# Moving a long convolution's x and result through memory channel by channel, with a deeper buffer for its inverse

## The chip, the cores and the metric

The program runs on one core of one Trainium2 chip. The metric is the device time of one execution in microseconds (us), as the median of several. The engines are TensorE (PE, matmuls; its weight loads are shown as PEld), VectorE (DVE), ScalarE (ACT), GpSimd (POOL) and SyncE (SP, which issues the DMAs here).

## The reference, cut to what matters

A long convolution gates its input, and two feed-forward layers follow it, token by token (S = 12480 tokens, D = 128 channels, FF = 2048):

```python
h = (relu(pos_emb @ w1) @ w2) * exp(-0.01 * pos)[:, None]
y = irfft(rfft(x * v, 2 * S) * rfft(h, 2 * S))[:S]      # over the tokens
t = x * y
h1 = t @ w_in1
P = a0 + a1 * h1 + a2 * h1**2 + a3 * h1**3
Q = 1 + abs(b0) * abs(h1) + abs(b1) * h1**2
t = (P / (Q + 1e-6)) @ w_out1
h2 = t @ w_in2
out = maximum(0.01 * h2, h2) @ w_out2
```

## The kernel before, in words

The first part (up to about 327 us) makes the transform of x * v and of h, multiplies them, and stores an intermediate `bd` in device memory. The second part, called the main part here, takes the last step of the inverse transform and both layers, tile by tile. A tile is five columns n of a 98 x 128 arrangement of the tokens, 490 or 486 tokens wide; tile 0 has three columns, 294 tokens; there are 26 tiles. In the main part a tile's numbers stand with the 128 channels on the partitions and the tokens along the row.

The steps of the main part have short names, and a table gives each to an engine:

- For each tile: `xP` (PE) transposes the tile's x from token rows (`xc`) into PSUM, five transposes; `xA` (ACT) copies it to SBUF. `yP` (PE) makes the inverse's result y with ten matmuls, each of which is two instructions in the trace, from `bt` (a part of `bd`) and the table `dt`; `yA` (ACT) copies it to SBUF. `yG` (POOL) multiplies x and y into `zf`; `zA` and `zG` split that into a high and a low part for three-pass matmuls. For tile 0 `yP` is called `wP`, and DVE does what POOL does for the others.
- Layer 1, for each of 16 blocks of 128 hidden units (a unit): `h1` (PE, three passes of one instruction each), then a chain over ACT, DVE and POOL that makes P / Q: `s`, `v`, `rho`, `r0` on ACT, `q`, `p`, `N` on POOL, `nn`, `d`, `ee`, `e`, `g` on DVE; `o1` (PE) adds the block to the tile's result. `g` is the chain's last step, and it is what `o1` waits for.
- Between the layers `uA`, `uB` (ACT) and `uG` (POOL) split the result of layer 1.
- Layer 2, for each of 16 units: `h2` (PE, three passes), `rl` (ACT), and `o2` (PE). In the four units that `CG` lists, `rh` (ACT) and `rg` (POOL) split the block and `o2` is done in three passes.
- At the end of a tile `oA` (ACT) copies the result to `o2s`; `oP` (PE) transposes it back in groups of four columns n, `oB` (ACT) copies that to `ot`, and SP stores token rows. There are 32 such groups.

The order on each engine is fixed before the program runs. `plan` (line 198) goes through the steps with a cost (`cost`, line 76) and a lag (`lag`, line 97) for each, and gives an engine that is free the ready step with the lowest number: the step's unit number plus its kind's entry in `PLACE` (line 55). `BUF` (line 47) has the number of buffers of each kind, and `work_list` (line 105) turns them into dependences. `h1`, `h2`, `xP`, `yP` and `oP` share three PSUM banks (`NHB`). Every engine then goes through its list in that order, and waits where an input isn't there. SP's DMAs stand in the order in which the steps that issue them come: the inputs of tile j + 2 are issued when both `xP` and `yP` of tile j have been recorded (`loaded`, line 928), since the buffers of `dt`, `xc` and `bt` are two each.

```python
def loaded(j, i):
    T["yin", j][i] = None
    if T["yin", j][0] is T["yin", j][2]:
        load_y(j + BUF["in"])
```

Of the kernel before, what the change touches and what calls it, by code (L numbers as in the profile page):

```python
# [75 lines left out]
def cost(k, w):  # L76
# [13 lines left out]
    if k in ("wP", "yP"):  # L90
        return w * 4.32
    if k == "xP":
        return w * 0.855
    return {"oP": 432, "oB": 478}[k]
# [10 lines left out]
def work_list(tiles):  # L105

    nt = len(tiles)
    off = [sum(tiles[:j]) for j in range(nt + 1)]
# [54 lines left out]
    for j in range(nt):  # L163
        w, b, n = COLS[j], j * NF, j * NF + NF - 1
        i = j - BUF["in"]
        load = [("xP", i, 7000), ("yP" if i else "wP", i, 7000)] if i >= 0 else []
# [8 lines left out]
        if j:
# [130 lines left out]
def conv_moe_moe(ctx: ExitStack, tc: tile.TileContext, I, out, dbg=None):  # L306
# [50 lines left out]
    xe, ve, oute = ends(x), ends(v), ends(out)  # L357

    with tc.manual_schedule():
# [549 lines left out]
        def load_y(j):  # L909
# [16 lines left out]
            T["yin", j] = [bt, dt, xc]

        def loaded(j, i):

            T["yin", j][i] = None  # L930
            if T["yin", j][0] is T["yin", j][2]:
                load_y(j + BUF["in"])

        def x_pe(j):
            t, xc = bank("xP", j), T["yin", j][2]
            for i in range(TILES[j]):
                c = cols(j, i)
                m = c.stop - c.start
                pe.transpose(t[:, c], xc[:m, i], ident[:m, :m])
            loaded(j, 2)  # L940
# [122 lines left out]
        def o_pe(b):
            t = bank("oP", b)
            for i in range(OB):
                n = b * OB + i
                j = max(k for k in range(len(TILES)) if OFF[k] <= n)
                c, m = cols(j, n - OFF[j]).start, ROW[n]
                pe.transpose(t[:m, i * D : (i + 1) * D], T["o2s", j][:, c : c + m], ident)

        def o_act2(b):
            n0 = b * OB
            ot = mp.tile([NU, OB, D], F32, tag="ot", name=f"ot{b}")
            m = ROW[b * OB]
            act.copy(ot[:m], T.pop(("oP", b))[:m].rearrange("p (i d) -> p i d", d=D))
            for sl, k, a, b in token_rows(n0, n0 + OB):
# [46 lines left out]
```

## Time and profile before

| | us |
|---|---|
| median of 3 runs | 1648.87 |
| lowest and highest run | 1644.95 and 1650.23 |
| the profiled execution, its own time | 1647.39 |
| the profiled execution, span from first to last instruction | 1645.6 |

The profile is of one execution. A busy PE in it is not PE at its peak: matmuls are pipelined and their ends are modelled, so a matmul's own duration is longer than the distance from its start to the next one's. This distance (the pitch) is what one instruction costs a PE that never waits.

### The profile page before, as it was taken

To read this page: it belongs to the slowest core of one execution; us is meant where nothing else is said; L and a number is where in the kernel's file an instruction comes from. 1 tells how busy PE (TensorE), PEld (TensorE's weight loads), DVE (VectorE), ACT (ScalarE), POOL (GpSimd) and SP (SyncE) were. 2 spreads that over 40 slices of the span, in tenths; PEclk is the share of its full clock that TensorE was granted. 3 is DMA by queue.
4 is the path that set the end of the run, shared out by engine and by line. 5 is a ranking of instruction groups with operands and counts; after the bars stand their busy time and mean duration, and the time that the engine had idled before them with its cause. 6 is when DMAs were issued, how large, how long until landed. Compare 5 with 4: busy or idle time off the path is not lost.

```text
span 1645.6 us, 21850 instructions
## 1 busy us (share of the span) xinstructions
PE 1588.4 (97%) x6568; PEld 1138.0 (69%) x6568; DVE 1459.0 (89%) x2401; ACT 1360.2 (83%) x2671; POOL 1391.5 (85%) x1187
## 2 busy tenths in 40 slices
PE   7889989888999999999999999999999999999998
PEld 5778888675666666666666666666666666666665
DVE  5878766579999999999999999999999999999991
ACT  4672483378999999999999999999999999999994
POOL 6637526588999999999999999999999999999992
PEclk9999999989999999999999999999999999999999
DMA  7846556541010111001110001110011110000000
GB/s 211 247 137 199 194 164 243 175 106 27 8 30 18 31 32 32 19 18 31 32 32 25 25 19 31 32 37 14 19 31 32 37 31 6 1 6 10 5 6 15
DMA packets 89048, 97.33 MB, mean 59 GB/s; under 512 B 53092, under 2 KB 58446, under 8 KB 87762
## 3 DMA queue, kind: packets, MB, share of 16 engines
q1 hardware_dynamic: 88010, 95.54, 19.9%
q8 instruction: 52, 0.85, 0.2%
q10 hardware_dynamic: 920, 0.40, 0.1%
q14 instruction: 66, 0.54, 0.1%
HBM read 70.84 MB, written 25.07 MB: 58 GB/s over the span
## 4 chain that ended last, share of the span: by engine, by line
PE 86%; DMA 5%; DVE 3%; POOL 2%; SPq 1%; issue 1%; ACT 1%; ACTq 0%; DVEq 0%; POOLq 0%
PE o1p L992 20%; PE o2p L992 15%; PE h L495 11%; PE h L497 11%; PE h L496 11%; PE xp L688 4%; PE yP L947 4%; PE gp L723 2%; PE ap L648 2%; PE gp L719 2%; DMA A<-x 1%; PE o2p L495 1%; PE o2p L497 1%; PE o2p L496 1%; DMA wk<-v 1%
## 5 line engine op out<-in xcount | busy, mean ns | idle before, releaser
L1028 POOL TENSOR_TENSOR wk<-wk 128x972 f32<-128x972 f32 (+2 forms) x208 | 470.0, 2260 | 23.7 <-DVE wk L1025 21.2
L992 PE MATMUL o1p<-g,wo 128*128 128x486 f32 (+2 forms) x832 | 405.6, 571 | 6.4 <-DVE g L1043 6.4
L1019 POOL TENSOR_SCALAR wk<-wk,pars 128x486 f32<-128x486 f32 (+2 forms) x416 | 314.3, 756 | 35.5 <-ACT wk L1011 20.8
L1030 DVE SCALAR_TENSOR_TENSOR v<-wk,absb,v 128x486 f32<-128x486 f32 (+2 forms) x416 | 297.1, 714 | 11.5 <-ACT v L1013 10.5
L1037 DVE SCALAR_TENSOR_TENSOR v<-v,r 128x486 f32<-128x486 f32 (+2 forms) x416 | 274.0, 659 | 33.3 <-ACT r L1035 30.7
L992 PE MATMUL o2p<-wk,wo 128*128 128x486 f32 (+2 forms) x624 | 301.6, 566 | 0.0
L1013 ACT ACTIVATE v<-h,absb 128x486 f32<-128x486 f32 (+2 forms) x416 | 267.4, 645 | 13.3 <-DVE g L1043 10.2
L1025 DVE TENSOR_TENSOR wk<-h,wk 128x486 f32<-128x486 f32 (+2 forms) x416 | 270.8, 651 | 0.5 <-POOL wk L1019 0.2
L1040 DVE SCALAR_TENSOR_TENSOR v<-v,r 128x486 f32<-128x486 f32 (+2 forms) x416 | 266.5, 659 | 4.7
L1011 ACT ACTIVATE wk<-h 128x486 f32<-128x486 f32 (+2 forms) x416 | 240.1, 577 | 35.4 <-PE h L497 29.5
L1033 ACT ACTIVATE rho<-v 128x486 f32<-128x486 f32 (+2 forms) x416 | 241.4, 580 | 24.0 <-DVE v L1030 23.4
L1035 ACT ACTIVATE r<-rho 128x486 f32<-128x486 f32 (+2 forms) x416 | 255.9, 615 | 3.6
L1043 DVE TENSOR_TENSOR g<-wk,v 128x486 f32<-128x486 f32 (+2 forms) x416 | 253.7, 649 | 4.0 <-POOL wk L1028 2.5
L495 PE MATMUL h<-zh,wh 128*128 128x486 f32 (+2 forms) x416 | 253.9, 610 | 3.3 <-DVE wk L1025 2.3
L1050 ACT ACTIVATE wk<-h 128x486 f32<-128x486 f32 (+2 forms) x416 | 242.0, 582 | 12.4 <-PE h L497 11.5
L1021 POOL TENSOR_SCALAR wk<-wk,pars 128x972 f32<-128x972 f32 (+2 forms) x208 | 239.6, 1152 | 0.0
L992 PEld LDWEIGHTS o2p<-wk,wo 128*128 128x128 f32 x624 | 117.8, 189 | 109.9 <-issue 104.6
L495 PE MATMUL h<-uh,wh 128*128 128x486 f32 (+2 forms) x416 | 187.6, 451 | 0.9 <-ACT wk L1050 0.9
L992 PEld LDWEIGHTS o1p<-g,wo 128*128 128x128 f32 x832 | 154.6, 191 | 47.0 <-issue 14.8
L497 PE MATMUL h<-zh,wl 128*128 128x486 f32 (+2 forms) x416 | 159.8, 384 | 0.0
L496 PE MATMUL h<-zl,wh 128*128 128x486 f32 (+2 forms) x416 | 159.7, 384 | 0.0
L497 PE MATMUL h<-uh,wl 128*128 128x486 f32 (+2 forms) x416 | 158.9, 382 | 0.0
(105 smaller groups left out, 2558.5 us busy)
## 6 DMA issues: line engine op xcount, KB each, us to landing
bd<-wk SPq DMA_DIRECT2D x44, 256.0 KB
bt<-bd SPq DMA_DIRECT2D x100, 112.5 KB
wk<-c_m SPq DMA_DIRECT2D x43, 256.0 KB
dt<-c_d SPq DMA_DIRECT2D x25, 344.5 KB
A<-x SPq DMA_DIRECT2D x32, 192.0 KB
wk<-v SPq DMA_DIRECT2D x32, 192.0 KB
out<-ot SPq DMA_DIRECT2D x32, 192.0 KB
xc<-x SPq DMA_DIRECT2D x25, 240.0 KB
```

Source lines behind the costliest of these rows:

```text
L495: pe.matmul(dst, w_h, z_h, start=start, stop=False)
L496: pe.matmul(dst, w_h, z_l, start=False, stop=False)
L497: pe.matmul(dst, w_l, z_h, start=False, stop=stop)
L992: pe.matmul(o, wo[l][:, f], T.pop((src, n))[:, :w], start=(f == 0), stop=(f == NF - 1))
L1013: act.activation(bank("v", n)[:, :w], one("h1"), AF.Abs, scale=kk)
L1019: pool.tensor_scalar(out=q, in0=sq, scalar1=a3, scalar2=a1, op0=ALU.mult, op1=ALU.add)
L1025: dve.tensor_tensor(out=half("nn"), in0=one("h1"), in1=two("q"), op=ALU.mult)
L1028: pool.tensor_tensor(out=nn, in0=nn, in1=T["p", n][:, : 2 * w], op=ALU.add)
L1030: dve.scalar_tensor_tensor(out=one("v"), in0=two("s"), scalar=bb, in1=one("v"), op0=ALU.mult, op1=ALU.add)
L1035: act.activation(mk("r0"), one("rho"), AF.Square)
L1037: dve.scalar_tensor_tensor(out=one("v"), in0=one("v"), scalar=C1, in1=one("r0"), op0=ALU.add, op1=ALU.mult)
L1040: dve.scalar_tensor_tensor(out=one("v"), in0=one("v"), scalar=-2.0, in1=one("r0"), op0=ALU.add, op1=ALU.mult)
```

## The change

x comes to the program a second time, as `xm`: 128 channels by 12480 tokens and a few columns of padding, in the order in which the tiles take them. The host writes this array before the launch, and puts the result, which now leaves as 128 channels by tokens in the same order, back into token rows after it. x as it was is still loaded for x * v in the first part.

So `xP`, `xA`, `oP` and `oB` are gone. A tile's x is one DMA straight into the buffer that `yG` reads (`xt`, three buffers), issued when `yG` of the tile three before is recorded; a tile's result is one DMA from `o2s`. The inputs `dt` and `bt` of tile j + 2 are issued right after `yP` of tile j. `yA` has 14 buffers in place of 4. The three-pass units of layer 2 are 0, 5, 7 and 13 in place of 1, 5, 9 and 13, and `PLACE` has other numbers.

```diff
+LEFT = [sum(COLS[:j]) for j in range(len(COLS) + 1)]
...
-    "s": 3, "q": 3, "p": 2, "nn": 3, "rho": 2, "r0": 3, "g": 3, "rl": 3, "rh": 2, "rd": 2, "zf": 2, "xA": 4, "yA": 4, "in": 2,
+    "s": 3, "q": 3, "p": 2, "nn": 3, "rho": 2, "r0": 3, "g": 3, "rl": 3, "rh": 2, "rd": 2, "zf": 2, "xA": 3, "yA": 14, "in": 2,
...
-CG = [1, 5, 9, 13]
+CG = [0, 5, 7, 13]
...
-    "N": -942.49, "d": -98.01, "e": 2053.67, "ee": -1296.06, "g": -1349.74, "go": -2822.11, "h1": -2.6, "h2":
+    "N": -5165.29, "d": -98.77, "e": 794.99, "ee": -3335.26, "g": -3628.59, "go": -7712.1, "h1": -2.6,
...
-    "P": "h1 h2 o1 o2 wP yP xP oP",
-    "A": "s v rho r0 rl rh yA xA zA uA uB oA oB",
+    "P": "h1 h2 o1 o2 wP yP",
+    "A": "s v rho r0 rl rh yA zA uA uB oA",
...
-        load = [("xP", i, 7000), ("yP" if i else "wP", i, 7000)] if i >= 0 else []
+        load = [("yP" if i else "wP", i, 7000)] if i >= 0 else []
...
-            op("yG", j, w, b, [("yA", j), ("xA", j)] + zf)
+            op("yG", j, w, b, [("yA", j)] + zf + ([("yG", j - BUF["xA"], 5000)] if j > BUF["xA"] else []))
...
-        op("oA", j, w, n + NF, [("o2", n)] + ([("oP", (off[j - 1] - 1) // OB)] if j > 1 else []))
+        op("oA", j, w, n + NF, [("o2", n)] + ([("oA", j - 2, 3000)] if j > 1 else []))
...
-                rows(xc, xr, xe, n0, n1, sp)
...
-        def x_pe(j):
...
+        def load_x(j):
+            if j < len(TILES):
+                T["xA", j] = mp.tile([128, TN * NU], F32, tag="xt", name=f"xt{j}", bufs=BUF["xA"]) if j else xt0
+                if j:
+                    sp.dma_start(T["xA", j][:, : COLS[j]], I["xm"][:, LEFT[j] : LEFT[j + 1]])
...
-            loaded(j, 0)
+            load_y(j + BUF["in"])
...
+            load_x(j + BUF["xA"])
...
-        def o_pe(b):
...
-        def o_act2(b):
...
+            sp.dma_start(out[:, LEFT[j] : LEFT[j + 1]], o)
...
+    arrays["xm"][:, col] = inputs["x"].reshape(S, D).T[:, tok]
...
+    out = nc.dram_tensor("out", (D, LEFT[-1]), F32, kind="ExternalOutput").ap()
...
+    res[tok] = r.results[0]["out"][:, col].T
```

How the order moves is seen at three places. In the names, `h1_16` is `h1` of unit 16, the first of tile 1, `yP_7` is `yP` of tile 7, and a number behind the second underscore means nothing.

PE at the start of tile 1, before:

```order
L497 MATMUL h1_15_2620<-zh0_2252,wl0_1722 128x294
L992 MATMUL o1p0_2370<-g10_2635,wo0_1724 128x294
L992 MATMUL o1p0_2370<-g11_2637,wo0_1724 128x294
L947 MATMUL yP_5_2656<-dt5_2555,bt5_2557 128x98 x10
L495 MATMUL h1_16_2677<-zh1_2361,wh0_1720 128x490
L496 MATMUL h1_16_2677<-zl1_2396,wh0_1720 128x490
L497 MATMUL h1_16_2677<-zh1_2361,wl0_1722 128x490
```

PE at the same place, in the change:

```order
L481 MATMUL h1_16_2662<-zh1_2352,wh0_1720 128x490
L482 MATMUL h1_16_2662<-zl1_2366,wh0_1720 128x490
L483 MATMUL h1_16_2662<-zh1_2352,wl0_1722 128x490
L920 MATMUL yP_7_2674<-dt7_2554,bt7_2555 128x98 x10
L966 MATMUL o1p0_2361<-g12_2700,wo0_1724 128x294
L966 MATMUL o1p0_2361<-g13_2702,wo0_1724 128x294
L920 MATMUL yP_8_2721<-dt8_2587,bt8_2588 128x98 x10
```

Two `yP` stand in the first unit of tile 1 where one stood just ahead of it, and they are those of tiles 7 and 8 where it was that of tile 5. In the whole list the change has `yP` 1 to 15 ahead of the last `g` of tile 2, and the list before has 1 to 7; from there both have one for each tile, up to `yP` 25.

SP in the stretch of these loads, before:

```order
L918 DMA dt4_2382<-c_d 90x980
L355 DMA xc4_2383<-x 96x640
L355 DMA xc4_2383<-x 2x640
L817 DMA bt4_2384<-bd_57 90x5x64 x4
L918 DMA dt5_2555<-c_d 90x980
L355 DMA xc5_2556<-x 96x640
L355 DMA xc5_2556<-x 2x640
L817 DMA bt5_2557<-bd_57 90x5x64 x4
L918 DMA dt6_2989<-c_d 90x980
L355 DMA xc6_2990<-x 96x640
L355 DMA xc6_2990<-x 2x640
L817 DMA bt6_2991<-bd_57 90x5x64 x4
```

SP in the same stretch, in the change:

```order
L903 DMA dt4_2337<-c_d 90x980
L803 DMA bt4_2338<-bd_57 90x5x64 x4
L903 DMA dt5_2417<-c_d 90x980
L803 DMA bt5_2418<-bd_57 90x5x64 x4
L913 DMA xt5_2440<-xm 128x490
L903 DMA dt6_2462<-c_d 90x980
L803 DMA bt6_2463<-bd_57 90x5x64 x4
L913 DMA xt6_2477<-xm 128x490
```

The rows of x in token order are gone from between `dt` and `bt`, and a tile's x is one row now, at a place of its own: it waits for `yG`, not for a step of PE.

PE at the end of the program, before:

```order
L497 MATMUL o2p25_15032<-rh413_15116,wol_1727 128x486
L992 MATMUL o2p25_15032<-wk_83,wo1_1725 128x486 x2
L1069 MATMUL oP_30_15139<-ident_63,o2s24_15005 97x128 x3
L1069 MATMUL oP_30_15139<-ident_63,o2s25_15137 97x128
L1069 MATMUL oP_31_15144<-ident_63,o2s25_15137 97x128 x4
```

PE at the end, in the change:

```order
L966 MATMUL o2p25_14563<-wk_83,wo1_1725 128x486 x2
L481 MATMUL o2p25_14563<-rh413_14619,woh_1726 128x486
L482 MATMUL o2p25_14563<-rd413_14635,woh_1726 128x486
L483 MATMUL o2p25_14563<-rh413_14619,wol_1727 128x486
L966 MATMUL o2p25_14563<-wk_83,wo1_1725 128x486 x2
```

The eight transposes behind the last `o2` are gone, and the last step on PE is `o2` itself.

## Rows read from the trace of the kernel before

**Rows 1.** The page, part 1: busy time of each engine.

```profile
PE 1588.4 (97%) x6568; PEld 1138.0 (69%) x6568; DVE 1459.0 (89%) x2401; ACT 1360.2 (83%) x2671; POOL 1391.5 (85%) x1187
```

**Rows 2.** Windows by stage: stretch, length, busy and count per engine, clock, DMA, GB/s.

```profile
327.00:373.00 46.00, 40.97 (x205) 34.23 (x205) 35.45 (x85) 34.33 (x83) 35.70 (x41) 0.80 0.46 106
373.00:422.10 49.10, 43.46 (x175) 28.82 (x176) 48.14 (x82) 43.15 (x87) 43.97 (x38) 0.93 0.09 23
422.10:471.30 49.20, 47.89 (x187) 32.19 (x186) 48.31 (x82) 44.94 (x89) 47.56 (x41) 1.00 0.06 15
471.30:1025.10 553.80, 553.79 (x2134) 374.49 (x2133) 528.66 (x880) 510.62 (x1005) 521.17 (x429) 1.00 0.10 27
1025.10:1374.80 349.70, 349.70 (x1360) 238.43 (x1360) 334.45 (x561) 322.98 (x640) 329.46 (x274) 1.00 0.10 27
1374.80:1422.30 47.50, 47.50 (x174) 31.68 (x174) 47.34 (x82) 45.41 (x91) 46.79 (x40) 1.00 0.02 5
1422.30:1565.30 143.00, 143.00 (x515) 95.00 (x515) 142.13 (x241) 136.16 (x269) 137.87 (x115) 1.00 0.02 6
1565.30:1611.80 46.50, 46.50 (x165) 30.51 (x164) 45.93 (x79) 42.80 (x84) 43.38 (x36) 1.00 0.02 5
1611.80:1645.60 33.80, 29.32 (x110) 19.46 (x108) 0.01 (x1) 15.28 (x28) 5.93 (x5) 1.00 0.06 18
```

**Rows 3.** Windows, line 1043 (g) alone: busy time of DVE and its count.

```profile
471.30:1025.10 553.80, 109.00 (x176) 1.00 0.10 27
```

**Rows 4.** PE in order of time: start, us from first to last, instruction.

```profile
888.23 1.04 PE L1069 MATMUL oP<-ident,o2s 128*98 128x128 f32 x8
889.11 0.99 PE L992 MATMUL o1p<-g,wo 128*128 128x490 f32 x2
...
902.21 0.58 PE L939 MATMUL xP<-ident,xc 97*128 97x97 f32 x5
902.64 1.01 PE L992 MATMUL o1p<-g,wo 128*128 128x490 f32 x2
...
910.14 2.37 PE L947 MATMUL yP<-dt,bt 90*128 90x97 f32 x20
912.29 0.47 PE L495 MATMUL h<-zh,wh 128*128 128x490 f32 x1
```

**Rows 5.** Groups by line: shape and count, busy us, mean ns, idle before.

```profile
L1069 PE MATMUL oP<-ident,o2s 128*98 128x128 f32 (+1 forms) x128 | 18.8, 274 | 0.3 <-ACT o2s L1061 0.3
L939 PE MATMUL xP<-ident,xc 98*128 98x98 f32 (+1 forms) x125 | 15.6, 258 | 0.7 <-DMA xc<-x 0.7
```

**Rows 6.** Windows of line 947 (yP, two), 939 (xP), 1069 (oP): PE, PEld.

```profile
327.00:422.10 95.10, 18.80 (x120) 18.08 (x120) 0.87 0.27 63
1025.10:1565.30 540.20, 16.59 (x140) 16.74 (x140) 1.00 0.07 20
1025.10:1565.30 540.20, 5.26 (x45) 4.75 (x45) 1.00 0.07 20
1025.10:1565.30 540.20, 8.30 (x56) 7.20 (x56) 1.00 0.07 20
```

**Rows 7.** DMA of 400 to 412 us: 40 slices of 0.3 us, and the whole.

```profile
GB/s 0 0 0 0 0 0 0 0 68 171 205 329 259 180 103 127 217 239 244 301 245 183 248 235 105 92 0 0 0 0 0 0 0 0 0 0 0 0 0 0
DMA packets 2081, 1.06 MB, mean 89 GB/s; under 512 B 1893, under 2 KB 1893, under 8 KB 2081
```

**Rows 8.** DVE in order of time, in the last tile.

```profile
1589.38 0.72 DVE L1030 SCALAR_TENSOR_TENSOR v<-wk,absb,v 128x486 f32<-128x486 f32 x1
...
1595.21 0.72 DVE L1030 SCALAR_TENSOR_TENSOR v<-wk,absb,v 128x486 f32<-128x486 f32 x1
```

**Rows 9.** All engines in order of time, at the end.

```profile
1640.04 0.56 ACT L1061 COPY o2s<-o2p 128x486 f32<-128x486 f32 x1 [1.66 <-PE o2p L992]
...
1641.04 1.07 ACT L1075 COPY ot<-oP 97x512 f32<-97x512 f32 x2 [0.44 <-PE oP L1069]
1641.65 1.39 SPq L1077 DMA_DIRECT2D out<-ot  x4
```

More of the change, by code (lines that the diff above doesn't have):

```diff
@@ L71 @@
 READ = {
-    "h1": "s v nn", "h2": "rl rh rd", "wP": "wD", "yP": "yA", "xP": "xA", "oP": "oB", "v": "g",
+    "h1": "s v nn", "h2": "rl rh rd", "wP": "wD", "yP": "yA", "v": "g",
 }
@@ L89, in cost @@
         return (2 if k == "N" else 1) * w * 2.1 + 150
[L90 to L94, printed above, removed]
+    return w * 4.32
 def lag(a, b):
@@ L107, in work_list @@
     nt = len(tiles)
-    off = [sum(tiles[:j]) for j in range(nt + 1)]
     ops = {}
@@ L184, in work_list @@
             op("wP", j, w, b, [])
-            op("wD", j, w, b, [("wP", j), ("xA", j)])
+            op("wD", j, w, b, [("wP", j)])
             op("zA", j, w, b, [("wD", j)])
@@ L811, in conv_moe_moe @@
         dt0 = wpool.tile([K1, TILES[0], 2, NU], F32, name="dt0")
-        xc0 = cut(wk, N2 * DG, [TILES[0], D])[:NU]
+        xt0 = cut(wk, N2 * DG, [COLS[0]])
         bt0 = cut(wk, N2 * DG + TILES[0] * D, [TILES[0], 2, D])[:K1]
@@ L843, in conv_moe_moe @@
                 sp.dma_start(dt0, I["c_d"][:, : TILES[0]])
-                rows(xc0, xr, xe, 0, TILES[0], sp)
+                sp.dma_start(xt0, I["xm"][:, : COLS[0]])
                 load_b(bt0, 0, 0, TILES[0])
@@ L918, in load_y @@
                 sp.dma_start(dt[:, :nn], I["c_d"][:, n0:n1])
-                rows(xc, xr, xe, n0, n1, sp)
-                nt = max(0, min(nn, NTAIL - n0))
-                if nt < nn:
-                    sp.dma_start(xc[NFULL:NU, nt:nn], xr[:1, n0 + nt : n1])
                 load_b(bt, 0, n0, n1)
             load_b(bt, 1, n0, n1)
[L926 to L932, printed above, removed]
-        def x_pe(j):
[L935 to L940, printed above, removed]
+            T["yin", j] = bt, dt
+        def load_x(j):
[3 more added lines that the diff above has]
+                    sp.dma_start(T["xA", j][:, : COLS[j]], I["xm"][:, LEFT[j] : LEFT[j + 1]])
         def y_pe(j):
-            t, (bt, dt, _) = bank("yP" if j else "wP", j), T["yin", j]
+            t, (bt, dt) = bank("yP" if j else "wP", j), T.pop(("yin", j))
             for i in range(TILES[j]):
@@ L1060, in o_act @@
             w = width(j)
-            act.copy(new("o2s", j, 1, F32, 2)[:, :w], T.pop(("o2", j))[:, :w])
-        def o_pe(b):
[L1064 to L1069, printed above, removed]
-        def o_act2(b):
[L1072 to L1076, printed above, removed]
-                sp.dma_start(oute[:, a:b] if k == "e" else outr[sl, a:b], ot[sl, a - n0 : b - n0])
+            o = new("o2s", j, 1, F32, 2)[:, :w]
+            act.copy(o, T.pop(("o2", j))[:, :w])
+            sp.dma_start(out[:, LEFT[j] : LEFT[j + 1]], o)
         work = {
@@ L1086, in conv_moe_moe @@
             "uB": lambda j: split("u", "f", j, T["o1", j][:, : width(j)]), "uG": lambda j: split("u", "l", j),
-            "oA": o_act, "oP": o_pe, "oB": o_act2, "wP": y_pe, "wD": w_dve,
+            "oA": o_act, "wP": y_pe, "wD": w_dve,
             "zD": lambda j: split("z", "l", j, en=dve),
         }
-        for j in range(BUF["in"]):
-            load_y(j)
+        for j in range(BUF["xA"] + 1):
+            if j < BUF["in"]:
+                load_y(j)
+            load_x(j)
         for k, i in order:
@@ L1099, with places @@
 _INS = ["x", "v", "pos_emb", "w1", "w2", "moe_w_in", "moe_w_out", "moe_a", "moe_b", "moe2_w_in", "moe2_w_out"]
+def places():
+    at = [(LEFT[j] + sum(ROW[sum(TILES[:j]) : n]), n) for j, t in enumerate(TILES) for n in range(sum(TILES[:j]), sum(TILES[: j + 1]))]
+    col = np.concatenate([c + np.arange(ROW[n]) for c, n in at])
+    tok = np.concatenate([n + N2 * np.arange(ROW[n]) for c, n in at])
+    return col, tok
 def bits(a):
@@ L1113 @@
     arrays.update(tables())
+    col, tok = places()
+    arrays["xm"] = np.zeros((D, LEFT[-1]), np.float32)
+    arrays["xm"][:, col] = inputs["x"].reshape(S, D).T[:, tok]
     aps = {
@@ L1121 @@
     r = run_bass_kernel_spmd(nc, [arrays], core_ids=[0])
-    return r.results[0]["out"]
+    res = np.empty((S, D), np.float32)
+    res[tok] = r.results[0]["out"][:, col].T
+    return res
```

16 lines of the change are left out of this document (2 added, 14 removed), and 8 rows, old and new, of the table PLACE.

## The prediction

> **What bounds the kernel now.** I read the busy times first, then the windows by stage, then single instructions of PE, and the DMAs last. PE is busy for 97% of the span, DVE for 89%, POOL for 85% [rows 1], but these are averages over two parts, so the stage decides. I cut the main part where tiles end: a tile has 16 g, and the stretch from 471.3 to 1025.1 us holds 176, eleven tiles [rows 3]. The stages are then tiles 0, 1, 2, then 3 to 13, 14 to 20, 21, 22 to 24, 25, and the tail [rows 2].
>
> From tile 2's end to tile 25's, PE has no idle time in any window, at a granted clock of 1.00, which is the level of 2.4 GHz. Tiles 3 to 13 take 50.35 us each (553.80 / 11) with DVE busy for 48.1 and POOL for 47.4; tiles 14 to 20 take 49.96 [rows 2]. That PE, and not its neighbours, sets this pace is shown by a change that the kernel makes by itself: it has no yP after tile 20 (140 instructions, seven tiles, in the stretch of tiles 14 to 24 [rows 6]), and tiles 21 to 24 take (47.50 + 143.00) / 4 = 47.6 us, 2.3 less. A yP costs PE 2.15 us by its pitch (910.14 to 912.29 [rows 4]). DVE's work for a tile is the same throughout; it was busy for 47.8 us of 49.96 and is busy for 47.3 of 47.5 [rows 2].
>
> So PE's time for a tile can be sold one for one until the tile takes what DVE or POOL need. Two units of DVE's chain in the last tile lie 5.83 us apart (1589.38 to 1595.21) [rows 8], 46.6 us for a tile's 16; POOL is busy for 46.8 us in tile 21 and for 46.0 each in 22 to 24 [rows 2]. The floor is about 46.6 to 47.
>
> **The Trainium skill, Trace Analysis, section Identifying the Most-Contended Engine** says that matmul busy time is a poor measure of how near TensorE is to its limit, and asks for weight loads' busy share, 69% here. By it DVE would be the first engine in tiles 3 to 13, and the change would move little; that is rival 3. The step from tile 20 to 21 speaks for PE.
>
> **The change, part by part.**
>
> *xP and oP leave PE.* Their mean durations are 258 and 274 ns [rows 5], but matmuls overlap, and the pitch is what PE gives up: five xP take 902.21 to 902.64, 0.43 us; eight oP take 888.23 to 889.11, 0.44 us for a group of four [rows 4]. All of them at the pitch make 26 x 0.43 + 32 x 0.44 = 25 us. I take the pitch, since the next matmul starts there. The Trainium skill, TensorE: Matmul & The Clock Gate, Part 4, gives about 275 ns for a transpose inside a kernel; the durations of the trace agree with that, and by it all 256 would make 70 us in place of 25.
>
> *Tiles 3 to 13* lose 11 x 0.43 + 14 x 0.44 = 10.9 us. One yP also leaves this stage, since yP 15 now stands ahead of tile 2's end: 2.15. Together 13.0, and a tile then takes 49.2, still over the floor, so I take all of it. If the neighbours eat one us of each tile, 2 are left.
>
> *Tiles 14 to 24* lose 9 xP (45 / 5) x 0.43 = 3.9, 14 oP groups (56 / 4) x 0.44 = 6.2, and the seven yP x 2.15 = 15.0 [rows 6]: 25.1 of 349.70 + 47.50 + 143.00 = 540.2, so 515.1 or 46.8 for a tile. There PE, DVE and POOL need the same within 1%, each in a fixed order, and I don't expect all three without a wait. Tiles 21 to 24 show 47.6 with PE just as full. I take the middle, 47.25: 11 x 47.25 = 519.8, a gain of 20.4. Bounds: 25.1 at PE's own pace, 16.3 if 47.63 stays (540.2 - 11 x 47.63).
>
> *The fourteen yA* let PE work ahead: yP 1 to 15 now stand before the end of tile 2, where 1 to 7 stood (six in tiles 0 and 1 [rows 6], one in tile 2). That brings 8 x 2.15 = 17.2 us into tiles 0 to 2 and takes five xP away, 2.2. PE is idle there for 46.0 - 41.0, 49.1 - 43.5 and 49.2 - 47.9, in all 12 us [rows 2]; in tile 0 DVE's chain fills up slowly (35.5 of 46.0) and PE's clock is at 0.80 of full, a mix of both levels. 15.0 us of new work against 12 of room: this stage gets 3 us longer. Bounds: 0, since a busy PE that waits or runs at the lower clock hides more room, and 15, if nothing fits.
>
> *Loads.* Each yP ahead needs its dt and bt. Here such a load, with xc beside it 1.06 MB in all, moved from 402.4 to about 407.8 us (slices 9 to 26), 5.4 us [rows 7]. The thirteen for yP 3 to 15 need 70 at most of the 144.3 that tiles 0 to 2 take, so I put no wait down. What a late load would hold up is in rival 4. xc stood ahead of bt on SP, behind xP's buffers; a tile's x is now one DMA of 128 rows that waits for yG, at no cost as long as yG runs ahead.
>
> *ACT* loses xA and oB, but it isn't full (510.62 of 553.80 [rows 2]); *the three-pass units* stay four for each tile. Both at nothing.
>
> *Tile 25* is at the floor already (46.5): nothing. *The tail* loses the oP group in its middle, 0.4, and the last stretch, where o2s starts at 1640.04, the copies to ot at 1641.04 (1.07), and SP issues four DMAs for 1.39 us [rows 9]: with one DMA behind o2s its issue starts at about 1640.65 and not 1641.65, and takes some 0.4 and not 1.4. I take 2.4 off; bounds 1 and 3.
>
> **Sum.** +3 - 13.0 - 20.4 - 2.4 = -32.8. The profiled execution took 1647.39 us: 1614.6. The median of the runs is 1.5 above it (1648.87); I say **1615 us**.
>
> **The rivals.** (1) *All three floors are reached*: tiles 0 to 2 take the yP for nothing and the late tiles run at 46.8. 0 - 13.0 - 25.1 - 2.4 = -40.5, 1607 us. For it speaks that tile 25 took 46.5 with PE full; against it, that tiles 21 to 24 did not. (2) *Work is moved and not hidden*: tiles 0 to 2 grow by all 15, and the late tiles stay at 47.63. +15 - 13.0 - 16.3 - 1 = -15.3, 1632 us. For it: PE is 97% busy in tile 2, where it overflows first. (3) *PE is not the bound*, the chain of DVE and POOL is, and the transposes were free: then only the tail moves, 1645 us, within 0.3% of before (4.9 us, about what a measurement of this kernel tells from no change). The step at tile 21 speaks against it. (4) *Slower: a yP at the head of PE's queue waits for its load.* PE goes in order, so h1 and o1 of the running tile stand behind it, and DVE's chain behind them. It is decided by the load's pace: thirteen loads would have to be late by (32.8 + 4.9) / 13 = 2.9 us each on PE to lose more than 0.3%, which needs (144.3 + 37.7) / 13 = 14.0 us for a load, against 5.4 measured. Then 1654 us.
>
> **How the numbers follow.** Forecast 0.50; rival 1 0.18; rival 2 0.24; rival 3 0.05; rival 4 0.03. Range: forecast with rivals 1 and 2, with 3 us outside each for bounds that add up, 1603 to 1634. Faster by over 0.3%: the first three and a part of rival 3's spread, 0.94; within 0.3%: 0.03; slower: 0.03.
>
> **What would show it.** Tiles 3 to 13 at 49.2 us each with PE full; tiles 14 to 24 at about 47.25 with PE, DVE and POOL all within 2% of full; last g of tile 2 near 474 us, with fifteen yP before it and PE's idle time there down from 12 to a few us; a tail of about 31.4. If tiles 3 to 13 stay over 50, PE was not the bound. If waits of yP on a DMA of bt or dt add up to more than 10 us, rival 4 is at work. If the late tiles take 48, the vector engines' order gives back what PE gained.

## The result, and the profile after

The changed kernel takes **1620.14 us** (median of 4 runs, 1615.31 to 1623.33), the kernel before beside it on the same chip 1649.55 us (4 runs, 1644.95 to 1653.09). The ratio is 0.9829, with a 95% interval of 0.9805 to 0.9852: 29.4 us off the median, where 32.8 were forecast.

The profiled execution took 1623.33 us, its span is 1621.5. The busy times of the page's part 1, which answer to [rows 1]:

```profile
PE 1568.3 (97%) x6312; PEld 1111.2 (69%) x6312; DVE 1450.2 (89%) x2401; ACT 1351.3 (83%) x2613; POOL 1389.2 (86%) x1187
```

PE has 256 instructions less, the transposes; its share of the span is the same, and those of the others are within one point. The page alone doesn't tell where the time went. For that the stages are cut again, each at the end of a tile's sixteenth g. They are counted from the start of wP, which lay between 320.9 and 328.9 us in the profiled executions of this study, before's 323.4 among them, so that this spread doesn't enter. The tile view of wP, first of before and then of after (the start of the first and of the last record stands behind the durations):

```profile
L947 PE MATMUL wP<-dt,wk x12: 421/421/531, 323.4 to 326.0; 90*128 90x98 f32 x12
```

```profile
L920 PE MATMUL wP<-dt,wk x12: 421/421/532, 328.9 to 331.6; 90*128 90x98 f32 x12
```

Windows of after by stage, with the columns of [rows 2]: tiles 0, 1, 2, then 3 to 13, 14 to 24, 25, and the tail.

```profile
328.90:377.80 48.90, 45.76 (x254) 40.72 (x255) 34.90 (x85) 31.93 (x79) 35.07 (x39) 0.79 0.77 178
377.80:429.40 51.60, 50.76 (x279) 40.12 (x278) 49.39 (x82) 45.90 (x96) 46.04 (x41) 1.00 0.55 121
429.40:476.90 47.50, 46.02 (x176) 30.76 (x175) 47.20 (x80) 44.60 (x88) 45.80 (x39) 1.00 0.11 26
476.90:1020.00 543.10, 543.10 (x2012) 362.89 (x2011) 525.30 (x882) 508.07 (x980) 520.35 (x430) 1.00 0.09 23
1020.00:1543.50 523.50, 520.97 (x1806) 336.12 (x1805) 520.61 (x881) 500.44 (x968) 513.35 (x427) 1.00 0.03 9
1543.50:1590.70 47.20, 46.98 (x161) 29.70 (x160) 46.41 (x78) 42.78 (x83) 43.41 (x36) 1.00 0.02 6
1590.70:1621.50 30.80, 27.10 (x95) 17.42 (x93) 0.02 (x1) 13.68 (x25) 5.96 (x5) 1.00 0.04 17
```

Beside before, from wP on, in us:

| stage | before | after | difference | forecast |
|---|---|---|---|---|
| tiles 0 to 2 | 147.9 | 148.0 | +0.1 | +3 |
| tiles 3 to 13 | 553.8 (50.35 each) | 543.1 (49.37) | -10.7 | -13.0 |
| tiles 14 to 24 | 540.2 (49.11) | 523.5 (47.59) | -16.7 | -20.4 |
| tile 25 | 46.5 | 47.2 | +0.7 | 0 |
| tail | 33.8 | 30.8 | -3.0 | -2.4 |
| sum | 1322.2 | 1292.6 | -29.6 | -32.8 |

The sum from wP on agrees with the medians. (The two spans differ by 24.1 only, since the profiled execution of after reached wP 5.5 us later.)

One thing has to be kept in mind where mid and late tiles are compared: tiles 1 to 12 are 490 tokens wide and tiles 13 to 25 are 486 (`COLS`), 0.8% less, which is up to 0.4 us of a tile. In before it shows between tiles that both have a yP: 50.4 us each for tiles 3 to 12 (471.3 to 975.0), 49.96 for tiles 14 to 20.

Where yP stands now shows in the windows of the tile yP alone (columns are PE, PEld, and ACT for its copy yA), for tiles 0 to 2, 3 to 13 and 14 to 24.

```profile
328.90:476.90 148.00, 40.29 (x300) 39.46 (x300) 8.49 (x15) 0.93 0.48 109
476.90:1020.00 543.10, 23.70 (x200) 23.91 (x200) 5.62 (x10) 1.00 0.09 23
1020.00:1543.50 523.50, 0.00 (x0) 0.00 (x0) 0.00 (x0) 1.00 0.03 9
```

Fifteen yP (300 of its records) stand in tiles 0 to 2, ten in tiles 3 to 13, none behind. The ten are in tiles 3 to 12; tile 13 has none. So ten mid tiles with a yP and the late tiles without one can be read against each other inside one kernel, with the 0.4 us for the width in mind. Tiles 3 to 12 of after:

```profile
476.90:971.80 494.90, 494.90 (x1843) 331.15 (x1842) 478.47 (x803) 461.68 (x890) 473.48 (x391) 1.00 0.09 24
```

They take 49.5 us each.

That the loads kept up is in the view of the tile yP between 328 and 480 us, in the list of what its engine waited for:

```profile
  DMA bt<-bd: 0.2, 1
```

One wait of 0.2 us. The end of the program, in order of time, answers to [rows 9]:

```profile
1617.84 0.56 ACT L1036 COPY o2s<-o2p 128x486 f32<-128x486 f32 x1 [1.65 <-PE o2p L966]
1618.43 0.33 SPq L1037 DMA_DIRECT2D out<-o2s  x1
```

From the start of the copy to the end of the span it is 1621.5 - 1617.84 = 3.7 us, where it was 1645.6 - 1640.04 = 5.6.

### The profile page after: what moved, and what is told of

Its sections match the earlier page's. It is cut to its first block, busy times and chain, and to the rows that moved or that the text cites. A ratio compares the mean times of both kernels' runs of the same rounds, so it can differ in the third digit from the quotient of the medians.

```text
span 1621.5 us, 21155 instructions
## 1 busy us (share of the span) xinstructions
PE 1568.3 (97%) x6312; PEld 1111.2 (69%) x6312; DVE 1450.2 (89%) x2401; ACT 1351.3 (83%) x2613; POOL 1389.2 (86%) x1187
## 4 chain that ended last, share of the span: by engine, by line
PE 56%; POOL 20%; DVE 10%; DMA 6%; issue 4%; ACT 3%; SPq 1%; POOLq 0%; ACTq 0%; DVEq 0%
PE o1p L966 12%; PE o2p L966 9%; POOL wk L1002 8%; PE h L481 7%; PE h L482 7%; PE h L483 7%; POOL wk L993 3%; PE yP L920 3%; PE xp L674 3%; POOL wk L995 3%; PE ap L634 2%; DVE v L1004 2%; PE gp L705 2%; DVE g L1017 2%; DVE wk L999 2%
## 5 line engine op out<-in xcount | busy, mean ns | idle before, releaser
L1002 POOL TENSOR_TENSOR wk<-wk 128x972 f32<-128x972 f32 (+2 forms) x208 | 470.2, 2261 | 41.1 <-DVE wk L999 30.6
L966 PE MATMUL o1p<-g,wo 128*128 128x486 f32 (+2 forms) x832 | 384.3, 570 | 1.5 <-DVE g L1017 1.1
L966 PE MATMUL o2p<-wk,wo 128*128 128x486 f32 (+2 forms) x624 | 297.4, 565 | 0.0
L987 ACT ACTIVATE v<-h,absb 128x486 f32<-128x486 f32 (+2 forms) x416 | 262.8, 645 | 21.5 <-DVE g L1017 18.8
L999 DVE TENSOR_TENSOR wk<-h,wk 128x486 f32<-128x486 f32 (+2 forms) x416 | 270.8, 651 | 2.4 <-POOL wk L993 1.0
L1024 ACT ACTIVATE wk<-h 128x486 f32<-128x486 f32 (+2 forms) x416 | 238.9, 575 | 23.0 <-PE h L483 12.1
L1007 ACT ACTIVATE rho<-v 128x486 f32<-128x486 f32 (+2 forms) x416 | 238.1, 572 | 20.8 <-DVE v L1004 13.1
L481 PE MATMUL h<-zh,wh 128*128 128x486 f32 (+2 forms) x416 | 247.4, 595 | 4.4 <-ACT rh L1026 3.1
L985 ACT ACTIVATE wk<-h 128x486 f32<-128x486 f32 (+2 forms) x416 | 238.4, 574 | 10.7 <-PE h L483 7.9
L481 PE MATMUL h<-uh,wh 128*128 128x486 f32 (+2 forms) x416 | 231.4, 556 | 0.7 <-DVE wk L999 0.7
L482 PE MATMUL h<-ul,wh 128*128 128x486 f32 (+2 forms) x416 | 158.3, 381 | 0.0
```

Source lines behind the costliest of these rows:

```text
L481: pe.matmul(dst, w_h, z_h, start=start, stop=False)
L482: pe.matmul(dst, w_h, z_l, start=False, stop=False)
L966: pe.matmul(o, wo[l][:, f], T.pop((src, n))[:, :w], start=(f == 0), stop=(f == NF - 1))
L987: act.activation(bank("v", n)[:, :w], one("h1"), AF.Abs, scale=kk)
L999: dve.tensor_tensor(out=half("nn"), in0=one("h1"), in1=two("q"), op=ALU.mult)
L1002: pool.tensor_tensor(out=nn, in0=nn, in1=T["p", n][:, : 2 * w], op=ALU.add)
```

## How full PE is, by its pitches

The busy time of PE is made of modelled ends, so I add up the pitches. PE in order of time in a mid tile of after, from a second pass on:

```profile
699.88 0.38 PE L482 MATMUL h<-ul,wh 128*128 128x490 f32 x1
700.10 0.38 PE L483 MATMUL h<-uh,wl 128*128 128x490 f32 x1
700.32 1.80 PE L966 MATMUL o1p<-g,wo 128*128 128x490 f32 x4
701.58 0.77 PE L481 MATMUL h<-zh,wh 128*128 128x490 f32 x1
702.18 0.38 PE L482 MATMUL h<-zl,wh 128*128 128x490 f32 x1
```

A pass of a three-pass product has a pitch of 0.22 us (699.88, 700.10, 700.32); the mean from the second pass to the third over tiles 3 to 12 is 0.223. The first pass behind o1 or o2 is stamped early and looks long; the sum across it is right: four records of o1 and one pass take 700.32 to 702.18, 1.86 us, so a record of o1 costs (1.86 - 0.22) / 4 = 0.41. A tile has 32 h and four o2 of three passes, 108 x 0.223 = 24.1; 16 o1 and 12 o2 of two records, 56 x 0.41 = 23.0; and a yP of 2.15 [rows 4]. That is 49.2 us with a yP, against 49.5 measured in tiles 3 to 12. Without a yP it is 47.1, or 46.7 at the late tiles' width (x 486 / 490, an estimate), against 47.59 measured. PE has next to nothing left in the mid tiles, and 0.9 us in the late ones. The experiments ask what that means.

## The experiments

Three questions: is it PE's work that sets the mid tiles, what sets the late ones, and which part of the change earned what. All runs are compared by the same cut into tiles. Windows of a run are those of tiles 3 to 13 and of 14 to 24, with the columns of [rows 2].

**1. Less work on PE.** The third pass of h2 is left out:

```
-            prod3(bank(...), wh, wl, T[p + "h", j], T[p + "l", j])
+            if l:
+                pe.matmul(t, wh[l][:, fs], T[p + "h", j][:, :w], start=True, stop=False)
+                pe.matmul(t, wh[l][:, fs], T[p + "l", j][:, :w], start=False, stop=True)
+            else:
+                prod3(t, ...)
```

> The changed kernel without the third pass of h2 (its product with the low part of the weights is left out): 16 x 0.22 = 3.5 us less PE work for each tile. Theory (DVE's chain sets the late tiles, PE the middle ones): tiles 14 to 24 stay between 47.1 and 47.6 us, tiles 3 to 13 fall from 49.4 to about 47.5. Rival (PE still sets the late tiles, as before the change): tiles 14 to 24 fall to about 44 to 45 us. Rival POOL: the same as the theory here, told apart by the next two runs.

Measured: 1615.43 us (one run; before beside it 1652.72).

```profile
472.90:1015.00 542.10, 534.31 (x1836) 315.18 (x1834) 524.99 (x882) 509.28 (x980) 519.75 (x430) 1.00 0.09 23
1015.00:1538.20 523.20, 507.93 (x1630) 289.83 (x1628) 520.48 (x881) 501.50 (x968) 513.05 (x427) 1.00 0.03 9
```

Sixteen passes, 3.5 us of PE's work, are gone from every tile, and tiles 3 to 13 take 49.28 us each in place of 49.37, the late ones 47.56 in place of 47.59. The late tiles came as forecast; the mid ones, forecast at 47.5, hardly moved. That PE's work alone sets the mid tiles is refuted. It also warns of the busy time: PE still reads 534 of 542 us, with 39 us of its work gone (176 records less, 0.223 each). The waits of its weight loads tell more. The list of waits between 500 and 950 us (in total, times, longest), of after, and then of this run:

```profile
PEld h L481 <- ACT wk L1024: 10.2, 39, 0.5
PEld h L481 <- DVE wk L999: 9.6, 34, 0.5
```

```profile
PEld h L481 <- DVE wk L1002: 38.8, 81, 1.0
PEld h L481 <- ACT wk L1027: 19.9, 51, 0.8
```

What PE saved it now waits in front of h1, for nn on DVE (L999, here L1002) and for the relu on ACT (L1024, here L1027), the last readers of the h banks that h1 is to fill.

**2. Less work on DVE, and on POOL.** In one kernel e is done on half of the columns, in the other N for one unit of each pair:

```
-                    out=one("v"), in0=one("v"), scalar=-2.0, in1=one("r0"), ...
+                    out=one("v")[:, :m], in0=one("v")[:, :m], scalar=-2.0, in1=one("r0")[:, :m], ...
```

```
-                nn = T["nn", n][:, : 2 * w]
-                pool.tensor_tensor(out=nn, in0=nn, in1=T["p", n][:, : 2 * w], op=ALU.add)
+                nn = T["nn", n][:, :w]
+                pool.tensor_tensor(out=nn, in0=nn, in1=T["p", n][:, :w], op=ALU.add)
```

> The changed kernel with e done on half of a unit's columns (the other half is left as it was): 16 x 0.25 = 4 us less DVE work for each tile. Theory (DVE sets the late tiles): tiles 14 to 24 fall from 47.6 to PE's 46.7 to 46.9 us, tiles 3 to 13 stay at 49.1 to 49.4. Rival (POOL sets them): tiles 14 to 24 stay within 0.2 us of 47.6. Rival (PE sets them): the same, within 0.2 us.

> The changed kernel with N done for one unit of each pair (half of the sum is left out): 8 x 1.0 = 8 us less POOL work for each tile. Theory (DVE sets the late tiles): tiles 14 to 24 stay within 0.3 us of 47.6, since g waits for N only now and then. Rival (POOL sets them): they fall to PE's 46.8.

Measured: 1613.31 us with less on DVE and 1614.63 with less on POOL, one run each. The windows of the first, then of the second:

```profile
467.90:1010.60 542.70, 542.70 (x2011) 364.15 (x2010) 492.26 (x881) 509.69 (x981) 521.62 (x430) 1.00 0.09 23
1010.60:1532.90 522.30, 519.92 (x1805) 337.56 (x1803) 486.47 (x881) 500.05 (x967) 513.88 (x427) 1.00 0.03 9
```

```profile
473.10:1015.70 542.60, 542.60 (x2012) 364.35 (x2011) 524.00 (x881) 509.22 (x980) 430.65 (x430) 1.00 0.09 23
1015.70:1534.90 519.20, 516.88 (x1805) 339.84 (x1804) 517.44 (x882) 499.18 (x968) 423.80 (x427) 1.00 0.03 9
```

DVE's busy time in the late tiles fell from 520.6 to 486.5 us, 3.1 a tile, and the tile from 47.59 to 47.48. POOL's fell by 8.1 a tile, and the tile to 47.20. Each is one profile, but where an edit left the late tiles alone they took 523.5 to 524.3 us in all in this study (the change, and the runs of experiments 3 and 4), so POOL's 4.3 us are clear and DVE's 1.2 hardly. So the amount of DVE's work doesn't set the late tiles, although DVE read as busy as PE; POOL's is worth 0.4 us there, between its two forecasts. In the mid tiles neither is worth anything (49.34 and 49.33), but PE, with all of its work, wouldn't have let those tiles fall by more than 0.3.

**3. More work on PE, in one block.** Twenty idle transposes ahead of each yP of tiles 16 to 25, which stand in tiles 3 to 12:

```
+            for k in range(4 if j > 15 else 0):
+                for i in range(TILES[j]):
+                    ...
+                    pe.transpose(t[:, c], wo[0][:m, i], ident[:m, :m])
```

> The changed kernel with 20 idle transposes of xP's shape ahead of each yP of tiles 16 to 25, into the bank that yP then overwrites; all ten lie in tiles 3 to 13. Theory (a transpose costs its pitch of 0.086 us): 1.7 us for each of these ten tiles, 49.4 to 51.1, in all 17 us. Rival (it costs its duration of 0.258 us): 5.2 us each, 54.5, in all 52 us. Rival (PE isn't the bound in these tiles): no change.

Measured: 1640.79 us, one run.

```profile
476.30:1036.50 560.20, 560.20 (x2211) 380.82 (x2210) 526.30 (x882) 509.60 (x980) 521.94 (x430) 1.00 0.09 22
1036.50:1560.80 524.30, 521.61 (x1806) 335.81 (x1805) 520.95 (x882) 501.09 (x968) 514.38 (x427) 1.00 0.03 9
```

The mid stage is 560.2 - 543.1 = 17.1 us longer, 0.086 for each of the 200 transposes, the pitch of [rows 4] (0.43 / 5), although a transpose lasts 247 ns in the mean of this run:

```profile
L921 PE MATMUL yP<-ident,wo 97*128 97x97 f32 (+1 forms) x200 | 18.5, 247 | 0.0
```

So the price by pitch is right, and work that PE gets in these tiles is paid in full. The Trainium skill, TensorE: Matmul & The Clock Gate, Part 4, gives about 275 ns for a transpose in one kernel's context; taken as the cost, 200 of them would be 55 us, an estimate from that page. This case's traces agree with it as a duration (247 to 274 ns), and show a third of it as the cost.

**4. More work on PE, in small pieces.** Adding costs everything and taking away earns nothing. One reading is that a block stops the fixed order, however full PE is. Here the same twenty transposes for a tile stand one or two ahead of each h1 of tiles 3 to 12:

```
+            if l == 0 and 3 <= j <= 12:
+                for i in range(2 if f % 4 == 0 else 1):
+                    pe.transpose(t[:, :98], wo[0][:98, f], ident[:98, :98])
```

> Idle transposes into h1's bank ahead of h1: two for every fourth unit, one for each other, twenty for a tile of tiles 3 to 12, so as many for a tile as were put ahead of each yP in the run with transposes in one block, where the ten tiles took 51.1 us each in place of 49.4 (1.71 more, 0.086 for one). Theory (it is the block that costs, since it stops the fixed order for longer than DVE has work in hand; PE's work in small pieces is covered): tiles 3 to 12 stay at 49.4, 49.7 at most, and the whole at 1621. Rival (PE is full in these tiles, every column that it is given costs its time wherever it stands): tiles 3 to 12 at 51.1, 17 us in all, about 1638.

Measured: 1638.8 us, one run.

```profile
471.00:1035.30 564.30, 564.30 (x2209) 378.50 (x2208) 529.54 (x881) 515.57 (x981) 521.66 (x430) 1.00 0.09 22
```

21.2 us longer, 0.106 for each. My theory of the block falls: scattered work costs no less. By the pitches PE needs 49.2 + 1.7 = 50.9 us in such a tile, so this is what a full PE asks for, and nothing covers more of it.

**5. The block in pieces, alone and with less work.** The yP of tiles 16 to 25 goes in four pieces with a unit of PE between two of them, and the numbers of `PLACE` are fitted anew to that; then the same with the edit of 1.

```
-            "yP": y_pe, ...
+            "yP": lambda j: y_pe(j, 0, 2 if j > 15 else 0), "yQ": lambda j: y_pe(j, 2, 3),
+            "yR": lambda j: y_pe(j, 3, 4), "yS": lambda j: y_pe(j, 4), ...
```

> The yP of tiles 16 to 25 in four pieces (two tokens, then one, one and one), with one h1, o1, h2 or o2 unit of PE between two pieces; the bank is held for some 5 us in place of 3, and the layers' order is fitted to it. Same work, fourteen buffers. Theory (a block of 2.15 us costs 1.8 because it is one block): tiles 3 to 12, which hold these pieces, fall from 49.4 to 48.0 or less, ten tiles of 1.4 or more, and the whole to 1607 or less. Rival (the work or the held bank costs it, not the block): tiles 3 to 12 stay at 49.4 within 0.3, or rise because the bank is held longer; 1618 to 1630.

> The last two edits together: yP of tiles 16 to 25 in four pieces, and the third pass of layer 2's product h2 left out (that part of the computation is not done), 16 x 0.22 = 3.5 us of PE's work less for a tile. Each alone left tiles 3 to 12 where they were (49.25 and 49.28 us). Theory (two limits stand at the same height in these tiles: PE's own work, 49.1 us by its pitches, and the stall that a yP in one block makes in the fixed order): with both lifted, tiles 3 to 12 fall to what tiles without a yP take, 47.5 to 48.0 each, 14 to 18 us less in all: 1598 to 1606. Rival (a yP stops the order in another way, by the h bank that it takes or by its yA and yG, which the pieces don't lift): tiles 3 to 12 stay at 49.0 to 49.4, 1614 to 1620. Tiles 14 to 24 at 47.6 under both.

Measured: 1618.66 us for the first (4 runs, 1617.76 to 1621.14; ratio to before 0.9814, 0.9797 to 0.983), which is not to be told from the change itself; 1610.51 for the second, one run. Tiles 3 to 13 of the first, then of the second, whose late tiles take 47.58:

```profile
472.40:1014.20 541.80, 541.80 (x2009) 362.96 (x2009) 524.98 (x880) 509.59 (x979) 519.12 (x429) 1.00 0.09 23
```

```profile
469.30:1009.90 540.60, 533.10 (x1832) 315.27 (x1831) 523.78 (x880) 508.23 (x978) 518.67 (x429) 1.00 0.09 23
```

49.25 and 49.15 us for a tile: my theory falls again, and the rival's range for a tile holds (1610.51 for the whole is below its 1614). So **two limits meet in a tile with a yP**, near 49.3 us. One is PE's work, 49.2 by its pitches: experiments 3 and 4 go over it. The other remains when 3.5 us of that work are gone, and it isn't the yP being one block. That it is the amount of DVE's or POOL's work, experiment 2 can't rule out here, since PE was full; but tiles without a yP hold the same work of both, and take 47.6, or 48.0 at the width of the mid tiles (x 490 / 486, an estimate). They take it with all of PE's work and with 3.5 us less alike, so it comes with a yP.

What a yP takes beside PE is one turn of the three h banks, and yA's 0.56 us on ACT. My guess was the banks: they are filled 32 times for a tile and 33 times with a yP, and 48.0 x 33 / 32 = 49.5, close to what tiles 3 to 12 take. Two rows speak against a mere count of turns. In tiles 21 to 24 of before, two xP and five oP groups fill the same three banks as well, and those tiles take what they take in the change without them. Before, then its xP (L939) and its oP (L1069) alone, then the change:

```profile
1374.80:1565.30 190.50, 190.50 (x688) 126.67 (x688) 189.47 (x322) 181.57 (x359) 184.66 (x154) 1.00 0.02 6
1374.80:1565.30 190.50, 1.17 (x10) 1.06 (x10) 1.00 0.02 6
1374.80:1565.30 190.50, 3.04 (x20) 2.64 (x20) 1.00 0.02 6
1353.10:1543.50 190.40, 189.49 (x657) 122.29 (x656) 189.33 (x321) 181.74 (x352) 184.63 (x154) 1.00 0.02 6
```

At 1.5 us for a turn (47.6 / 32) the seven more would have cost 10. And a yP in pieces holds its bank longer, here for 5.1 us up to its copy, where it is 2.7 in the change, and the tiles didn't grow:

```profile
L922 PE MATMUL yP<-dt,bt x20: 248/275/275, 563.2 to 567.6; 90*128 90x97 f32 x16, 90*128 90x98 f32 x4
L929 ACT COPY yA<-yP x1: 556/556/556, 568.3 to 568.3; 128x486 f32<-128x486 f32 x1
```

So what the second limit is stays open. No run took the banks or yA away: every version has three banks for h, three for e, and one each for o1 and o2.

**6. The parts of the change.** The change with the order and the three-pass units of before, and with fourteen buffers:

```
-CG = [0, 5, 7, 13]
+CG = [1, 5, 9, 13]
 PLACE = {
-    "N": -5165.29, "d": -98.77, "e": 794.99, ...
+    "N": -942.49, "d": -98.01, "e": 2053.67, ...
```

> The changed kernel, fourteen yA, with the numbers of PLACE and CG from before. Theory (most of the gain is PE work that is gone, and PE's total is the same here): 0 to 6 us slower than the change, tiles 3 to 13 at 49.2 to 49.6. Rival (the new numbers carry the gain): 15 us or more slower than the change.

Measured: 1629.47 us (4 runs, 1627.23 to 1631.33; ratio 0.9877, 0.986 to 0.9894; before beside it 1649.49, 11 runs).

```profile
473.20:1016.80 543.60, 543.60 (x2028) 365.51 (x2027) 529.27 (x882) 499.17 (x981) 520.02 (x430) 1.00 0.11 27
1016.80:1550.40 533.60, 527.12 (x1866) 344.21 (x1866) 525.34 (x880) 499.88 (x972) 512.86 (x427) 1.00 0.03 10
```

Between the two forecasts: the layout and the buffers earn 20.0 us, the new order with its three-pass units 9.3 more. By the stages it is 10.1 us in the late tiles (48.51 against 47.59), where with the order of before three yP still stand (x1866 against x1806, 60 records). At the 1.5 us of experiment 7 they are about half of that; the rest isn't told apart.

**7. Four buffers.** Two kernels with four buffers for yA and yP's place of before, one with the change's order, one with that of before:

```
-    ..., "xA": 3, "yA": 14, "in": 2,
+    ..., "xA": 3, "yA": 4, "in": 2,
...
-    "yP": -193.98, ...
+    "yP": -138.73, ...
```

> The changed kernel with four yA, as before, and yP's entry in PLACE at its old -138.73 (with -193.98 the order can't be laid out on four). yP then stand some nine tiles ahead and not twelve: about three yP, 6.5 us of PE work, come back from tiles 0 to 2 into later tiles where PE sets the pace. Theory (the deep buffer is worth what PE's early idle time takes in): 3 to 7 us slower than the change. Rival (the yP ahead cost tiles 0 to 2 as much as they save later): within 1 us or faster. Tiles 0 to 2 then take 3 to 6 us less than in the change.

> x and the result channel by channel alone: four yA, PLACE and CG as before. Theory: 25 us of PE work less (26 x 0.43 + 32 x 0.44) and a shorter tail, so 24 to 28 us of the change's 29.4. Rival (the buffer and the order carry half): 15 us or less.

Measured: 2075.25 us (4 runs, 2071.02 to 2080.00; ratio 1.2581, 1.2554 to 1.2607) and 2084.57 (4 runs; 1.2631, 1.2607 to 1.2656), a quarter slower than before, which neither forecast had. Windows of the first: a stretch inside tile 3, one in tile 4, then tiles 3 to 13:

```profile
545.00:590.00 45.00, 31.63 (x76) 16.47 (x74) 24.31 (x38) 22.84 (x40) 20.99 (x19) 0.83 0.06 14
600.00:620.00 20.00, 17.67 (x58) 10.29 (x57) 16.82 (x28) 16.92 (x33) 17.23 (x15) 1.00 0.04 13
516.10:1363.20 847.10, 660.94 (x2022) 370.06 (x2020) 560.87 (x881) 536.76 (x978) 522.28 (x429) 0.93 0.07 18
```

Tiles 3 to 13 take 77 us each. What happens is in the view of the tile yP of this run, in three stretches: yP 11, yP 12 with yA 11, and yA 12.

```profile
L920 PE MATMUL yP<-dt,bt x20: 275/275/352, 466.5 to 468.7; 90*128 90x98 f32 x20
...
L920 PE MATMUL yP<-dt,bt x20: 275/275/352, 540.6 to 542.8; 90*128 90x98 f32 x20
L925 ACT COPY yA<-yP x1: 562/562/562, 590.6 to 590.6; 128x490 f32<-128x490 f32 x1
...
L925 ACT COPY yA<-yP x1: 568/568/568, 666.3 to 666.3; 128x490 f32<-128x490 f32 x1
```

The order lays yP far ahead, but its copy to yA has to wait until one of the four buffers is read. Till then the result lies in an h bank: yP 11 from 466.5 to 590.6, yP 12 from 540.6 to 666.3, some 125 us each, where it is 3 us in the change. In tiles 3 to 13 one bank or two of the three are blocked at any time. With two blocked, PE is busy for 31.6 of 45 us, and with one for 17.7 of 20 (the yP of tile 13 starts at 621). The largest waits of PE's weight loads, in total over the run, are those of h for nn, which reads an h bank:

```profile
PEld h L481 <- DVE wk L999: 236.9, 217, 3.0
```

So banks held this long stall the order, though it is a far larger scale than one turn. In before the same place was harmless: there yP stands only some five tiles ahead (yP 16 starts at 910 us [rows 4], in tile 11). By `work_list` that is because its load also waited for xP, whose copy waited for x's buffers; no run tried this by itself.

So these two don't measure what the buffers are worth. A third does, with four buffers and an order fitted to them, in which yP stands two or three tiles ahead:

> Four buffers for the inverse's result as before, x and the result channel by channel as in the change, and an order fitted to four buffers, in which yP stands two to three tiles ahead (yP 25 in tile 23), so no yP waits in a bank for a buffer. Theory (the fourteen buffers earn what the late tiles gain, since only they let yP stand in tiles 0 to 2): one yP in each of tiles 3 to 23; tiles 3 to 13 at 49.4, tiles 14 to 23 at 49.4 in place of 47.6, and tiles 0 to 2 at most 5 us shorter: 1633 to 1640. Rival (a yP costs its time wherever it stands, and tiles 0 to 2 get back what the late tiles lose): tiles 0 to 2 at 132, late tiles at 49.4, 1621 within 4.

Measured: 1629.25 us (4 runs, 1627.04 to 1629.35; ratio 0.9876, 0.9859 to 0.9892). Tiles 0 to 2, 3 to 13, 14 to 24:

```profile
322.60:464.90 142.30, 126.18 (x494) 88.58 (x495) 129.65 (x245) 118.25 (x252) 125.69 (x116) 0.92 0.20 48
464.90:1008.60 543.70, 543.53 (x2021) 359.89 (x2020) 530.26 (x882) 508.24 (x979) 520.83 (x430) 1.00 0.11 27
1008.60:1546.90 538.30, 538.28 (x2006) 359.19 (x2005) 526.38 (x880) 502.45 (x979) 515.98 (x428) 1.00 0.08 21
```

9.1 us slower than the change by the medians, between the two forecasts. The late tiles, now with a yP in ten of eleven, take 48.94 (14.8 us more in all), and tiles 0 to 2, with four yP in place of fifteen, are only 5.7 us shorter. A yP costs 1.5 us late (14.8 / 10) and 0.5 early (5.7 / 11): that difference is what the buffers buy (the rest of the order is fitted anew too, so it is not a price to the tenth).

**8. yP spread over more tiles.** The change's order, with the yP of tiles 16 to 25 standing 1.9 tiles apart, in tiles 5 to 22:

```
-            op("yP", j, w, b, ...)
+            op("yP", j, w, b if j < 16 else 16 * (3 + 1.9 * (j - 15)) - PLACE["yP"], ...)
```

> The changed kernel with yP of tiles 16 to 25 laid 1.9 tiles apart, from tile 5 to tile 22, and not one in each of tiles 4 to 13. Theory (DVE leaves PE some 0.9 us free in every late tile, and PE alone sets tiles 3 to 13): the late tiles with a yP go to at most 48.9, those without stay at 47.5, the sum of tiles 3 to 24 falls by 5 to 10 us. Rival (a yP costs its 2.15 us wherever it stands, since the chain can't catch up between two of them): no change, within 1 us.

Measured: 1640.05 us (6 runs, 1635.11 to 1644.65; ratio 0.9936, 0.9919 to 0.9953), some 20 us slower than the change.

```profile
474.40:1013.50 539.10, 536.14 (x1912) 350.69 (x1911) 528.09 (x883) 504.95 (x975) 521.11 (x430) 1.00 0.07 19
1013.50:1562.40 548.90, 536.48 (x1907) 348.53 (x1906) 527.25 (x882) 500.27 (x974) 515.30 (x428) 1.00 0.05 13
```

Both forecasts missed. Five yP have moved from the mid tiles to the late ones. The mid tiles got back 4.0 us, the late ones gave 25.4, and PE has waits of its own there now. Spreading doesn't help in this order. Why the late tiles lost so much more than five yP stays open: the longest, tile 23 with 52.6 us, has no yP at all. The rest of the order is a schedule that was fitted to the other places, and wasn't fitted anew here.

## Why the prediction was right, and where not

The time, 1620.14, lies in the range of 1603 to 1634, and the terms have the right signs and an order of size. By its own steps:

- **xP and oP by the pitch**: confirmed. Tiles 3 to 13 gave 10.7 us of 13.0, and twenty transposes more cost 1.71 us, 0.086 each. By their durations in the trace (258 and 274 ns [rows 5]) the 256 transposes would have given some 68 us.
- **PE as the bound of tiles 3 to 13**: confirmed for work that is added (17.1 and 21.2 us for 200 transposes), and by the sum of pitches, 49.2 of 49.5. By this rival 3 falls. But the proof that the prediction gave for it, the step at tile 21, doesn't hold by itself: with 3.5 us of PE's work gone from every tile, the tiles with a yP are still 1.7 us longer than those without (49.28 and 47.56, up to 0.4 of it their width). A yP costs time in another way too. The Trainium skill, Perfetto Trace Analysis, section Identifying the Most-Contended Engine, calls matmul busy time a bad measure, and experiment 1 agrees (534 of 542 us with 39 us of work gone). For the weight loads' share, which it asks for beside the share of peak arithmetic, this case disagrees: 363 of 543 us, 67%, with PE full.
- **"PE's time for a tile can be sold one for one until the tile takes what DVE or POOL need"**: this step failed, without much harm here. The next limit of a tile with a yP isn't DVE's 46.6 but some 49.3, just where the change ended. Experiment 1 took 39 us more from PE in tiles 3 to 13; down to 46.6 this step would have promised some 30 of them, and 1.0 came.
- **Tiles 14 to 24 at 47.25, the middle between 46.8 and 47.63**: mis-sized. They take 47.59, the bound that tiles 21 to 24 of before had already shown, and the gain was 16.7, not 20.4. I expected waits among three full engines, but thought that they would shrink. Less work on PE or DVE leaves 47.6 and 47.5, less on POOL 47.2, so none of the three sets it by its work alone; ACT's wasn't tried, and what sets it stays open.
- **Tiles 0 to 2, +3**: they got 0.1 longer. The fifteen yP fit better than 12 us of idle time allowed for: PE's idle time there fell from 12 to 5.5 us (48.90 - 45.76, 51.60 - 50.76, 47.50 - 46.02), its granted clock in tile 1 was 1.00 where it had been 0.93 [rows 2], which fits the room that the lower bound had allowed for, and a yP there costs 0.5 us by experiment 7. Rival 2 thus failed in this term, although its late tiles came true.
- **Loads at nothing, rival 4**: yP waited for a DMA for 0.2 us in all.
- **The tail, -2.4**: -3.0, within its bounds; the end behind o2s is 1.9 us shorter by itself. Tile 25 lost 0.7.

The forecast thus was 3.2 us too good in the sum (-32.8 against -29.6), nearly all of it in the late tiles (3.7) and the mid ones (2.3), with tiles 0 to 2 making up for 2.9. The late tiles' gain also needed the new order, to which the prediction gave no term of its own: with the old one, and three yP among them, they take 48.51.

No version here that does all of the work clearly beats the change: that with yP in pieces is level with it.

## What to carry to other kernels

Add up pitches to see whether an engine is full, and then ask both ways on the chip: twenty idle instructions show whether more of its work costs time, and a pass left out shows whether less would earn any. In a kernel tuned this far the answers differ, because several limits have been brought to the same height. And an order that lays a product far ahead needs a buffer for it beyond PSUM: where its copy has to wait, it blocks a bank that the running work needs.

## What was unexpected

A stage can lose PE work and hardly any of PE's busy time: with 39 us less in tiles 3 to 13, the profile reads 534 of 542 us busy, since a record lasts longer than its pitch (0.38 us against 0.22) and so covers a short wait behind it. And the clock fell with the banks: in the stretch of 545 to 590 us with two banks blocked, PE was busy for 31.6 of 45 us and its granted clock was 0.83 of the full 2.4 GHz in the mean, a mix of both levels, against 1.00 in every stage of the change behind tile 0.
